# Two entries of an attention step's order exchanged: scores ahead of transposes, on one Trainium2 core

## The chip, the core and the metric

The kernel runs on one core of a Trainium2 chip. The metric is device time in microseconds of one execution, from launch to end; lower is better. Engines are named as in the profile: PE is TensorE, with PEld for its weight loads, DVE is VectorE, ACT is ScalarE, POOL is GpSimd, and SP is the engine that issues DMAs.

## What is computed

An attention with a hash mask, followed by a mixture of four two-layer networks over all rows (cut to what matters):

```python
batch, n_heads, seq, head_dim = 2, 8, 768, 64
q_bits = (q @ proj > 0); k_bits = (k @ proj > 0)          # 6 bits each
mask = q_bucket[:, :, :, None] == k_bucket[:, :, None, :]  # same 6-bit bucket
scores = where(mask, scale * q @ k.T, -1e9)
attn = exp(scores - max) / (sum + 1e-9)
x = (attn @ v), heads side by side                        # 1536 x 512
for e in range(4):
    out += p[:, e:e+1] * (relu(x @ w1[e]) @ w2[e])        # 512 -> 1024 -> 512
```

## The kernel before

**Stages.** The attention of batch 0 runs first and alone (8 heads, about the first 125 us). After it the networks run on batch 0's rows, with the attention of batch 1 spread between their matmuls, and last the networks on batch 1's rows.

**A head** has 768 rows, in 6 steps of 128 rows each. In the text, step t of head h is one of steps 0 to 5, and heads of batch 0 are 0 to 7, with head 8 the first of batch 1. One pass of the loop `for i in range(...)` in `attention()` handles step i and also late stages of earlier steps, each given by one letter of the string `ORDER`:

- **S** (`stage_s`, L447 and L449 on PE): the scores of step i, four matmuls into a double PSUM bank `sps`, of which there are two; then on DVE the row minimum and copy into the SBUF tile `p` (L454).
- **E** (`stage_e`, L470 on ACT): the exponential of step i-1, in place in `p`.
- **T** (`stage_t`, L515 on PE): the six 128x128 transposes of the tile `p` of step i-3, three into each of two PSUM banks `ptps`. ACT copies the first bank to SBUF (L521); the second is copied by DVE (L519) in steps 0, 2, 3 and 5, by ACT in steps 1 and 4. There are four single banks, shared with `pv` and `hps` below, and a bank is written again when its last reader is done. Only batch 0's heads have this stage.
- **X** and **Y**: batch 1's way to transpose, on DVE and by DMA.
- **V** (`stage_v`, L565 on PE): attention times v of the head before, one half (12 matmuls) in step 3 and one in step 5; **U** copies the result `pv` out, ACT (L592) for one half and DVE (L590) for the other, in step 2.
- **N**, **R**, **M**: the row sums' reciprocals (L481, L482 on DVE), their way through DRAM, and on POOL the scaling by them (in steps 3 and 4 of every odd head, L603 to L608).
- **P**: the preparation of the next head. Step 1: `ah` on ACT (L376) and from it three copies on POOL (L265). Step 2: `al` on DVE (L379) and from it a POOL copy `ah<-al` (L265). Step 3: hash matmuls `hps` on PE (L391), their signs on ACT (L401), then on POOL `al<-k` (L406) and `k<-al` (L265), which the first scores of the next head read.

The code is emitted in this order, and each engine executes its own instructions in the order in which they were emitted:

```python
for i in range(n + LAG_M[1] + 3):
    for op in ORDER:
        c = do(op, i)
        if c is not None:
            yield c
```

`T` and `S` each end with a `yield`. While batch 0's attention runs alone, the caller counts the yields, and on some of them puts in a piece of the split of the first weights (a DVE cast, L755, and a POOL subtraction, L745).

Of the kernel before, what the change touches and what calls it, by code (L numbers as in the profile page):

```python
# [42 lines left out]
W_SPLIT = 40  # L43
W_STEP = 6
PREP_AT = 0
ORDER = "TXSUVMEYNRP"
LIGHT_FROM = 8
DRAIN = 2000
SPLIT_FIRST = 3
# [7 lines left out]
def tile_lsh_attention__then__domain_moe(  # L57
# [570 lines left out]
    def attention():  # L628
# [76 lines left out]
# [3 lines that stand above are left out]
# [509 lines left out]
```

## Time and profile before

| | |
|---|---|
| median of 3 runs | 703.48 us (703.40 to 703.51) |
| the profiled execution | 703.57 us, of which its span is 701.9 us |
| PE busy | 695.0 us (99%) |
| DVE, ACT, POOL busy | 515.3, 330.9, 307.5 us |
| TensorE clock granted | 0.999 of full speed |

The span runs from the first to the last instruction; the rest of the time lies around it. A busy share is an average over stages. PE's ends of matmuls are modelled, so PE's waits are better read from the distance between the starts of its groups than from its busy time.

### The profile page before, as it was taken

Reading aid. Unit: us, or ns where it says so; the run is one execution under the profiler, and the core shown is the slowest. Engines: PE = TensorE matmul, PEld = TensorE weight load, DVE = VectorE, ACT = ScalarE, POOL = GpSimd, SP = SyncE. Lnnn points to the kernel's source line nnn. Section 1 sums busy time; section 2 is a strip of 40 time slices with the busy share of each in tenths; the row PEclk is TensorE's granted clock in tenths of the full one; section 3 lists DMA queues with packets and bytes.
Section 4 is the critical chain, followed back from the end, with each engine's and each line's share of the span. In section 5 each row is a group of like instructions: output and inputs, shape, how many; then the busy total and the mean of one; then the engine's idle time right before and its main releaser. Section 6 shows DMA issues by size and latency. Waiting matters only on the chain.

```text
span 701.9 us, 10122 instructions
## 1 busy us (share of the span) xinstructions
PE 695.0 (99%) x3702; PEld 589.4 (84%) x3702; DVE 515.3 (73%) x839; ACT 330.9 (47%) x646; POOL 307.5 (44%) x290
## 2 busy tenths in 40 slices
PE   8999999999999999999999999999999999999998
PEld 7766675878878878877998989899898989989896
DVE  6898898967678568785768786777767667776762
ACT  7887788544543553551424444343333424343330
POOL 6359578623443543461525555342423324232420
PEclk9999999999999999999999999999999999999999
DMA  5323444669979778684221222411123121112202
GB/s 140 67 49 75 88 105 80 233 168 295 253 224 306 219 249 296 215 289 140 60 77 52 83 70 81 149 62 62 62 87 90 50 71 61 61 60 91 81 11 90
DMA packets 83938, 87.77 MB, mean 125 GB/s; under 512 B 52400, under 2 KB 54960, under 8 KB 81840
## 3 DMA queue, kind: packets, MB, share of 16 engines
q1 hardware_dynamic: 82864, 86.79, 41.4%
q8 instruction: 29, 0.48, 0.3%
q10 hardware_dynamic: 1024, 0.33, 0.2%
q14 instruction: 21, 0.17, 0.1%
HBM read 65.04 MB, written 22.07 MB: 124 GB/s over the span
## 4 chain that ended last, share of the span: by engine, by line
PE 94%; DVE 2%; POOL 2%; issue 1%; ACT 1%; DMA 0%; POOLq 0%; DVEq 0%
PE mps L786 13%; PE mps L788 12%; PE mps L787 12%; PE mps L1070 8%; PE mps L1074 8%; PE mps L1073 8%; PE pv L565 8%; PE sps L447 4%; PE sps L449 4%; PE ptps L515 4%; PE mps L836 3%; PE mps L838 3%; PE mps L837 3%; PE hps L391 1%; DVE p L454 1%
## 5 line engine op out<-in xcount | busy, mean ns | idle before, releaser
L786 PE MATMUL mps<-w2hi,hh 128*128 128x512 f32 (+1 forms) x388 | 150.6, 388 | 0.0
L788 PE MATMUL mps<-w2hi,hl 128*128 128x512 f32 (+1 forms) x388 | 150.3, 387 | 0.0
L787 PE MATMUL mps<-w2lo,hh 128*128 128x512 f32 (+1 forms) x388 | 150.3, 387 | 0.0
L1056 POOL TENSOR_TENSOR w2lo<-ws,w2hi 128x512 fp32r<-128x512 f32 x48 | 61.2, 1298 | 148.4 <-ACT w2hi L1055 146.9
L454 DVE TENSOR_SCALAR_CACHE_REDUCE p<-sps 128x768 f32<-128x768 f32 x96 | 90.3, 941 | 27.8 <-PE sps L449 26.1
L470 ACT ACTIVATE p<-p,nb 128x768 f32<-128x768 f32 x96 | 89.5, 932 | 24.1 <-DVE p L454 23.7
L780 DVE SCALAR_TENSOR_TENSOR acc<-mps,pe,acc 128x512 f32<-128x512 f32 (+1 forms) x85 | 63.0, 741 | 45.6 <-PE mps L788 45.2
L1074 PE MATMUL mps<-xo,w1lo 128*128 128x384 f32 x272 | 91.4, 336 | 0.0
L1073 PE MATMUL mps<-xo,w1hi 128*128 128x384 f32 x272 | 91.3, 336 | 0.0
L1070 PE MATMUL mps<-xo,w1hi 128*128 128x384 f32 x272 | 91.3, 336 | 0.0
L1080 ACT ACTIVATE hh<-mps 128x384 fp32r<-128x384 f32 x96 | 47.3, 492 | 92.5 <-PE mps L1074 62.9
L788 PEld LDWEIGHTS mps<-w2hi,hl 128*128 128x128 f32 x388 | 72.9, 188 | 15.2
L786 PEld LDWEIGHTS mps<-w2hi,hh 128*128 128x128 f32 x388 | 72.9, 188 | 14.5 <-issue 0.6
L787 PEld LDWEIGHTS mps<-w2lo,hh 128*128 128x128 f32 x388 | 72.9, 188 | 14.0
L1100 DVE TENSOR_TENSOR mt<-mps,mt 128x384 f32<-128x384 f32 x72 | 40.2, 558 | 45.2 <-PE mps L1074 44.4
L1014 POOL TENSOR_TENSOR w1lo<-ws,w1hi 128x512 fp32r<-128x512 f32 x36 | 49.5, 1378 | 44.3 <-ACT w1hi L1010 17.1
L565 PE MATMUL pv<-pt,tv 128*64 128x384 f32 x288 | 67.1, 492 | 0.0
L1085 DVE SCALAR_TENSOR_TENSOR hl<-mps,hh 128x384 fp32r<-128x384 f32 x96 | 53.4, 556 | 14.7 <-ACT hh L1080 12.4
L1010 ACT ACTIVATE w1hi<-wc 128x512 fp32r<-128x512 f32 x48 | 30.0, 630 | 66.6 <-DVE wc L1019 66.6
L265 POOL TENSOR_SCALAR q<-ah 64x768 fp32r<-64x768 f32 (+1 forms) x33 | 27.1, 822 | 76.2 <-ACT ah L376 61.9
L447 PE MATMUL sps<-ah,q 128*128 128x384 f32 x192 | 54.0, 362 | 0.4 <-DVE p L454 0.4
L534 DVE STREAM_TRANSPOSE t<-p 128x768 f32<-128x768 f32 x48 | 46.2, 964 | 8.5 <-ACT p L470 8.3
(137 smaller groups left out, 1372.2 us busy)
## 6 DMA issues: line engine op xcount, KB each, us to landing
ws<-in_moe_w_dram SPq DMA_DIRECT2D x64, 512.0 KB, 3.8
scr<-t SPq DMA_DIRECT2D x16, 1152.0 KB, 8.0
pt<-scr SPq DMA_DIRECT2D x16, 1152.0 KB, 6.8
tv<-in_v_dram SPq DMA_DIRECT2D x16, 192.0 KB, 5.9
tqk<-in_q_dram SPq DMA_DIRECT2D x30, 96.0 KB, 3.6
out_dram<-acc SPq DMA_DIRECT2D x11, 256.0 KB, 2.0
tqk<-in_k_dram SPq DMA_DIRECT2D x28, 96.0 KB, 3.7
rdb<-row SPq DMA_DIRECT2D x14, 192.0 KB, 4.5
```

The lines of the kernel that those rows point to most:

```text
L447: nc.tensor.matmul(ps[:, i, :NH], q1[:, sl], k1[:, i * NH : (i + 1) * NH], start=True, stop=False)
L454: nc.vector.tensor_scalar(out=two(pt), in0=ps[:, :, :NH], scalar1=MASKED, scalar2=MASKED, op0=ALU.min, op1=ALU.min, accum_out=nb,)
L470: nc.scalar.activation(pt, pt, ACTF.Exp, bias=nb, scale=-1.0, accum_out=dens[b, h, r][:, o : o + 1])
L565: nc.tensor.matmul(dst, vvs[b, h][:, c], pts[b, h, g][c], start=c == 0, stop=c == NT - 1, tile_position=(0, g * D),)
L780: nc.vector.scalar_tensor_tensor(out=acc, in0=ps, scalar=pcol, in1=acc, op0=ALU.mult, op1=ALU.add)
L786: nc.tensor.matmul(ps, hh[:, ts], w2hi[:, f, cs], start=n == 0, stop=False)
L787: nc.tensor.matmul(ps, hh[:, ts], w2lo[:, f, cs], start=False, stop=False)
L788: nc.tensor.matmul(ps, hl[:, ts], w2hi[:, f, cs], start=False, stop=n == FC - 1)
L1056: nc.gpsimd.tensor_tensor(out=lo[:, c + o], in0=t[:, o], in1=hi[:, c + o].bitcast(F32), op=ALU.subtract)
L1070: nc.tensor.matmul(ps, whi[:, kk, fs], xh[kk], start=first and kk == 0, stop=False, skip_group_check=True)
L1073: nc.tensor.matmul(ps, whi[:, kk, fs], xl[kk], start=False, stop=False, skip_group_check=True)
L1074: nc.tensor.matmul(ps, wlo[:, kk, fs], xh[kk], start=False, stop=kk == KH - 1, skip_group_check=True)
```

## The change

The two letters T and S change places, by way of X: in each step the scores of the step now come ahead of the transposes of the tile three steps behind.

```diff
 PREP_AT = 0
-ORDER = "TXSUVMEYNRP"
+ORDER = "XSTUVMEYNRP"
 LIGHT_FROM = 8
```

Batch 1's heads have no T, and X stands ahead of S in both strings, so nothing moves there but at the border between the two batches. ACT's and POOL's instructions stand in the same order before and after, SP's too.

On PE, this is the second half of attention times v in step 5 (its last matmul), and steps 0 and 1 of the next head; before:

```order
L565 MATMUL pv<-pth,tv 64x384
L515 MATMUL ptps<-ident,p 128x128 x6
L447 MATMUL sps<-ah,q_538 128x384 x2
L449 MATMUL sps<-k_541,al 128x384 x2
L515 MATMUL ptps<-ident,p 128x128 x6
L447 MATMUL sps<-ah,q_538 128x384 x2
L449 MATMUL sps<-k_541,al 128x384 x2
```

and now:

```order
L565 MATMUL pv<-pth,tv 64x384
L447 MATMUL sps<-ah,q_538 128x384 x2
L449 MATMUL sps<-k_541,al 128x384 x2
L515 MATMUL ptps<-ident,p 128x128 x6
L447 MATMUL sps<-ah,q_538 128x384 x2
L449 MATMUL sps<-k_541,al 128x384 x2
L515 MATMUL ptps<-ident,p 128x128 x6
```

After attention times v PE had the transposes first; now it has the first scores of the new head first. The same holds behind the hash matmuls of step 3.

On DVE, this is the stretch from step 2 of a head (its minimum, L454) over the copy out of `pv` and the preparation of the next head (L590 to L379) to steps 3 and 4; before:

```order
L519 COPY pth<-ptps 128x3x128
L454 TENSOR_SCALAR p,nb<-sps 128x768
L590 COPY xr<-pv 64x384
L481 TENSOR_SCALAR den<-den 128x6
L482 RECIPROCAL rd<-den 128x6
L379 SCALAR_TENSOR_TENSOR al<-xt,qk_scale,ah 128x768
L519 COPY pt<-ptps 128x3x128
L454 TENSOR_SCALAR p,nb<-sps 128x768 x2
```

and now:

```order
L454 TENSOR_SCALAR p,nb<-sps 128x768 x2
L519 COPY pth<-ptps 128x3x128
L590 COPY xr<-pv 64x384
L481 TENSOR_SCALAR den<-den 128x6
L482 RECIPROCAL rd<-den 128x6
L379 SCALAR_TENSOR_TENSOR al<-xt,qk_scale,ah 128x768
L454 TENSOR_SCALAR p,nb<-sps 128x768
L519 COPY pt<-ptps 128x3x128
```

The copies L519 of steps 2 and 3 now stand behind the minimum L454 of their step.

## Rows read from the trace of the kernel before

**Rows 1.** Span, clock; then a window's length, busy PE, PEld, DVE, ACT, POOL, clock, DMA.

```profile
core 0: 701.9 us, clock 0.999
...
125.00:650.00 525.00, 525.00 (x2703) 460.44 (x2700) 381.90 (x589) 217.38 (x413) 213.58 (x173) 1.00 0.44 141
```

**Rows 2.** Timeline of PE in head 6: start, length, instructions merged.

```profile
86.70 0.87 PE L515 MATMUL ptps<-ident,p 128*128 128x128 f32 x6
87.33 0.59 PE L447 MATMUL sps<-ah,q 128*128 128x384 f32 x2
87.76 0.51 PE L449 MATMUL sps<-k,al 76*128 76x384 f32 x2
88.11 0.82 PE L515 MATMUL ptps<-ident,p 128*128 128x128 f32 x6
88.69 0.60 PE L447 MATMUL sps<-ah,q 128*128 128x384 f32 x2
...
91.55 0.59 PE L447 MATMUL sps<-ah,q 128*128 128x384 f32 x2
...
92.42 0.54 PE L565 MATMUL pv<-pt,tv 128*64 128x384 f32 x1
...
94.41 0.81 PE L391 MATMUL hps<-xt,pf 128*44 128x384 f32 x4
95.15 1.04 PE L515 MATMUL ptps<-ident,p 128*128 128x128 f32 x6
...
98.24 0.54 PE L565 MATMUL pv<-pt,tv 128*64 128x384 f32 x1
...
100.33 0.87 PE L515 MATMUL ptps<-ident,p 128*128 128x128 f32 x6
```

**Rows 3.** Timeline of ACT in head 6, brackets: idle time ahead.

```profile
87.28 0.49 ACT L521 ACTIVATE pth<-ptps 128x384 f32<-128x384 f32 x1 [1.19 <-PE ptps L515]
...
91.14 0.49 ACT L521 ACTIVATE pth<-ptps 128x384 f32<-128x384 f32 x1
91.52 0.48 ACT L592 ACTIVATE xr<-pv 64x384 f32<-64x384 f32 x1
```

**Rows 4.** Timeline of DVE in head 6, steps 2 and 3.

```profile
92.64 0.56 DVE L590 COPY xr<-pv 64x384 f32<-64x384 f32 x1
...
93.47 1.54 DVE L379 SCALAR_TENSOR_TENSOR al<-xt,qk_scale,ah 128x768 fp32r<-128x768 f32 x1
95.03 0.56 DVE L519 COPY pt<-ptps 128x384 f32<-128x384 f32 x1
```

**Rows 5.** Timeline of POOL: pieces of the preparation in heads 3, 5, 6, 7.

```profile
59.15 0.83 POOL L265 TENSOR_SCALAR k<-al 12x768 fp32r<-12x768 f32 x1
...
80.92 0.83 POOL L265 TENSOR_SCALAR ah<-al 64x768 fp32r<-64x768 f32 x1 [0.96 <-DVE al L379]
...
85.88 0.83 POOL L265 TENSOR_SCALAR k<-al 12x768 fp32r<-12x768 f32 x1
...
94.28 1.42 POOL L265 TENSOR_SCALAR k<-ah 64x768 fp32r<-64x768 f32 x1
...
113.47 0.83 POOL L265 TENSOR_SCALAR k<-al 12x768 fp32r<-12x768 f32 x1
```

**Rows 6.** Timeline: PE transposes at heads' starts, and ACT's copy before batch 0's last product.

```profile
17.57 0.88 PE L515 MATMUL ptps<-ident,p 128*128 128x128 f32 x6 [0.61 <-ACT p L470]
...
44.82 0.87 PE L515 MATMUL ptps<-ident,p 128*128 128x128 f32 x6
...
60.49 0.82 PE L515 MATMUL ptps<-ident,p 128*128 128x128 f32 x6
...
72.71 0.88 PE L515 MATMUL ptps<-ident,p 128*128 128x128 f32 x6
...
113.89 0.88 PE L515 MATMUL ptps<-ident,p 128*128 128x128 f32 x6
...
119.75 0.47 ACT L521 ACTIVATE pth<-ptps 128x384 f32<-128x384 f32 x1
```

## The prediction, made before the changed kernel ran

> **What bounds the kernel now.** I read the table of stages first. From 125 us to 650 us PE is busy for all of the 525 us, at a granted clock of 1.00 [rows 1], so what is gained or lost ahead of 125 us moves the end by as much. Batch 1's order does not change, so the whole question lies in the first 125 us, batch 0's attention.
>
> Next I read the timeline of PE in one head there, by the distance between starts. Write S0 and T0 for the scores and transposes of a head's step 0, and so on. A T takes 0.58 us up to the scores behind it (88.11 to 88.69), and 0.63 when it comes after attention times v (86.70 to 87.33). An S takes 0.78 up to a T (87.33 to 88.11) and 0.87 up to attention times v (91.55 to 92.42). The halves of attention times v take 1.99 (92.42 to 94.41) and 2.09 (98.24 to 100.33), the hash 0.74 [rows 2]. The head's instructions cost 4 x 0.58 + 2 x 0.63 + 4 x 0.78 + 2 x 0.87 + 4.08 + 0.74 = 13.26 us, and the head lasts 13.63 (86.70 to 100.33). So PE sets the pace with some 0.4 us of waits. One of them stands in T4, which begins at 95.15: its second bank is still being copied out by DVE until 95.59, while its first three transposes take only 0.29 us [rows 2, 4].
>
> Then I read the other engines for how near they are. ACT waits 1.19 us for T0 behind attention times v, copies at 87.28, and from there works without a break to the copy of T2, which ends at 91.63 [rows 3]. The first half of attention times v reads that copy; it starts at 92.42 [rows 2], 0.79 us later. That is all the room ACT has. DVE ends `al` at 95.01 and copies step 3's bank right behind it [rows 4]. POOL's last preparation `k<-al` ends at 59.98, 86.71 and 114.30 in heads 3, 5 and 7 [rows 5].
>
> **The change, step by step.** No instruction is added or removed; 48 groups of transposes, and their DVE copies, move behind one group of scores. What this costs in a head, from the moment at which PE leaves the head before (time 0):
>
> *PE alone.* T now goes ahead of attention times v and S behind it. I price T up to attention times v as 0.58 plus the 0.09 that S pays there, and an S behind attention times v or the hash as 0.78 plus the 0.05 that T pays there. The sum is again 13.26: the move itself is free.
>
> *ACT starts later.* S0 takes 0 to 0.83, so T0 starts at 0.83, and ACT's first copy 0.58 behind (86.70 to 87.28) at 1.41, where it was 0.58 [rows 2, 3]. ACT waited there already, so nothing absorbs this. The copy of T2 ends 4.35 later (87.28 to 91.63), at 5.76, and PE can go on about 0.06 after. PE itself arrives at 3 x (0.78 + 0.58) + 0.05 + 0.78 + 0.67 = 5.58. Attention times v begins at 5.82: a **wait of 0.24**.
>
> *DVE's copy of step 3 is later.* ACT's half of the copy of `pv` ends at 1.41 + 4.72 = 6.13 (92.00 less 87.28) and DVE's half starts after it, at 6.2 [rows 3]. `al` starts 0.83 to 1.1 after that (0.83 in the row), takes 1.54, and now a minimum of 0.88 comes between it and the copy of 0.55, which ends near 10.1 [rows 4]. PE leaves attention times v at 7.81 and the hash at 8.55, does S4 in 0.83, and needs that bank for T4's second half at 9.67. I take a **wait of 0.45**; 0 if DVE's steps keep their old times, 0.9 if a cast falls among them. The head then lasts 13.26 + 0.24 + 0.45 = **13.95**, against 13.63.
>
> *POOL's preparation is later, and is wanted sooner.* POOL's first copies need ACT's `ah`, which moves by 0.83. They then run into `al` on DVE: the copy that starts at 94.28, inside `al` (93.47 to 95.01), takes 1.42 and ends 0.69 after it, while its like takes 0.83 [rows 4, 5]. With `al` ending near 8.7, `k<-ah` ends near 9.4, and `ah<-al` starts there, not at 80.92 less 72.71, 8.21, as in head 5 [rows 5, 6]: 1.2 later. Behind it stands a fixed queue on POOL up to `k<-al`. In the odd heads it holds the scaling by the row sums too, and `k<-al` ended at 15.16, 14.00 and 13.97 (heads 3, 5, 7, from rows 5 and the starts in [rows 6]). Now it ends at 16.4, 15.2, 15.2, and the next head's S0 asks for it at 13.95 + 0.43 = 14.38 (its L449 stands 0.43 behind L447 [rows 2]), since no transposes stand ahead of it. **Waits of 2.0, 0.8 and 0.8.** Behind them T0 has still to run, where it used to fill part of the time. In even heads the queue is shorter and ends with room.
>
> The SBUF page of the Trainium skill ("SBUF — State Buffer", Who interferes with whom) gives a rule for this: DVE and GpSimd share one pair of ports as an exclusive lock, and a DVE instruction with two SBUF inputs holds it until it ends. The 1.42 agrees with it nearly; by the rule alone the blocked copy would take its full 0.83 after `al`, which makes the three waits 0.14 longer each and the sum 0.4 us larger.
>
> *Beginning and end.* In head 1 T0 waited 0.61 us for an exponential [rows 6]; S0 now goes there. I take -0.5 (0 to -0.6). At the end, batch 0's last product waits for the copy that ends at 120.22 [rows 6], at the end of an ACT queue that starts with T0 of head 8 and so moves by 0.8 again: +0.7 (0 to 0.8).
>
> **Sum.** Even heads 2, 4, 6: 3 x 0.32 = +0.96. Head 3, up to the point where S0 and T0 of head 4 are done: 13.95 + 2.0 + 1.41 less 15.67 (44.82 to 60.49) = +1.7. Head 5: 13.95 + 0.8 less 13.99 (72.71 to 86.70) = +0.8. Head 7: 13.95 + 0.8 less 13.56 (100.33 to 113.89) = +1.2 [rows 2, 6]. Beginning -0.5, end +0.7. Together **+4.8 us**. The profiled execution took 703.57, the median is 703.48, less than 0.1 apart, so I forecast 708.3.
>
> **Rivals.**
> *Faster: the waits of T go, and nothing takes their place.* A tile has one S more of time until it is transposed, which covers the waits for exponentials and copies. The same skill's page on traces ("Perfetto Trace Analysis", Optimization Strategy) tells one to find the gaps of the most contended engine and make what they wait for complete sooner, which this order does for T. With no waits, five heads fall by 0.37 each, head 5 by 0.73, head 4's start by 0.6, the beginning by 0.5: -3.7, 699.8. It comes out so if ACT ends T2's copy before PE has come to attention times v; against it, ACT has 0.79 us of room and is put back by 0.83 against PE's clock, and PE arrives earlier by 0.14. Chance 0.09.
> *No change.* New waits of about 0.4 us per head and a POOL that is not late, since in heads 6 and 7 its queue is full and not `ah` sets its times: 703.5, within 0.2% either way. For it speaks that the move itself is free; against it, head 3's `k<-al` was already late in the old order. Chance 0.13.
> *Slower by more.* DVE's casts and `al` block POOL oftener, and the delays of one head reach into the next: another 3 us or so, 711.5. Chance 0.10.
> That the change does nothing is excluded: PE's and DVE's rows are in another order.
>
> **Numbers.** The forecast's chance is 0.68. Its low end: even heads 0.1 better than before, `ah<-al` late by ACT's 0.83 alone (odd heads +1.3, +0.4, +0.8), beginning -0.6, end 0: +1.5, about 705. Its high end: 0.5 us more in each of six heads and no gain at the beginning: +8.3, 711.8. The range 704.0 to 711.3 leaves out the faster case (0.09), the part of the unchanged one below 704.0 (0.07) and an upper edge (0.04). A measurement of this kernel tells 0.2%, 1.4 us, from no change; so slower by more than that 0.78, within it 0.13, faster 0.09.
>
> **What would show it.** In the profile after, ACT's idle time for T0 behind attention times v should be near 2.0 us and not 1.19; PE should wait for ACT's copy at the first half of attention times v, for DVE's copy in T4, and for POOL's `k<-al` at S0 of heads 4, 6 and 8, by 2.0, 0.8, 0.8; heads 2, 4 and 6 should last about 13.95; and the windows behind 125 us should be the old ones, moved. I am wrong if heads last under 13.6, or if POOL is done in time: that is decided by whether POOL's first copies wait for `ah` or for POOL's own queue.

## The result and the profile after

| | before | after |
|---|---|---|
| median of 5 runs | 703.51 us (703.40 to 703.69) | 708.13 us (708.01 to 708.46) |
| span of the profiled execution | 701.9 us | 706.3 us |

The ratio is 1.0066, 95% interval 1.0051 to 1.0081: the change makes the kernel 4.6 us slower.

The window behind 125 us in the kernel after comes first, as in [rows 1]: its length, then busy time and count of PE, PEld, DVE, ACT and POOL, the granted clock, DMA share and rate. Below it stands the first matmul of the networks, after and then before.

```profile
125.00:650.00 525.00, 525.00 (x2700) 458.02 (x2697) 382.51 (x592) 217.91 (x415) 215.61 (x175) 1.00 0.44 140
...
129.83 0.44 PE L836 MATMUL mps<-xs,w1hi 128*128 128x384 f32 x1
...
125.44 0.44 PE L836 MATMUL mps<-xs,w1hi 128*128 128x384 f32 x1
```

The window reads as it did: PE full, clock 1.00. The first matmul of the networks begins at 129.83 us where it began at 125.44. These 4.4 us are the whole growth of the span, so all of the loss is in batch 0's attention.

Next is PE's timeline in head 6 of the kernel after, which answers to [rows 2] (start, length, instructions merged, and in brackets idle time and its releaser).

```profile
89.06 0.62 PE L447 MATMUL sps<-ah,q 128*128 128x384 f32 x2
...
90.07 0.82 PE L515 MATMUL ptps<-ident,p 128*128 128x128 f32 x6
...
94.14 0.49 PE L515 MATMUL ptps<-ident,p 128*128 128x128 f32 x3
94.99 0.55 PE L515 MATMUL ptps<-ident,p 128*128 128x128 f32 x3 [0.36 <-ACT pth L521]
...
99.01 0.83 PE L515 MATMUL ptps<-ident,p 128*128 128x128 f32 x6
99.59 0.60 PE L447 MATMUL sps<-ah,q 128*128 128x384 f32 x2
...
103.22 0.61 PE L447 MATMUL sps<-ah,q 128*128 128x384 f32 x2
```

The head lasts 14.16 us (89.06 to 103.22) against 13.63 before. T0 begins 1.01 us behind the head's start, 0.20 of it a wait of S0 for POOL (shown below for head 4). T3 now breaks in two: its second half has to wait until ACT has copied the bank that it goes to. T4 runs through here; in most of the heads it waits.

The same head on ACT and then on DVE, which answers to [rows 3, 4].

```profile
90.60 0.49 ACT L521 ACTIVATE pth<-ptps 128x384 f32<-128x384 f32 x1 [2.03 <-PE ptps L515]
...
94.45 0.49 ACT L521 ACTIVATE pth<-ptps 128x384 f32<-128x384 f32 x1
94.83 0.48 ACT L592 ACTIVATE xr<-pv 64x384 f32<-64x384 f32 x1
```

```profile
95.40 0.56 DVE L590 COPY xr<-pv 64x384 f32<-64x384 f32 x1
...
96.23 1.54 DVE L379 SCALAR_TENSOR_TENSOR al<-xt,qk_scale,ah 128x768 fp32r<-128x768 f32 x1
97.80 0.96 DVE L454 TENSOR_SCALAR_CACHE_REDUCE p<-sps 128x768 f32<-128x768 f32 x1
...
98.68 0.55 DVE L519 COPY pt<-ptps 128x384 f32<-128x384 f32 x1
```

ACT waits 2.03 us for T0 where it waited 1.19. Its copy out of `pv` ends at 95.31, and DVE's copy out of `pv` starts right behind it, 6.34 us into the head (5.94 before). So `al` starts 7.17 us into the head, where it was 6.77. After `al` the minimum comes first and step 3's copy second.

Last, the first scores of head 4, on PE and on POOL.

```profile
59.80 0.62 PE L447 MATMUL sps<-ah,q 128*128 128x384 f32 x2
61.44 0.62 PE L449 MATMUL sps<-k,al 76*128 76x384 f32 x2 [1.02 <-POOL k L265]
```

```profile
60.55 0.83 POOL L265 TENSOR_SCALAR k<-al 12x768 fp32r<-12x768 f32 x1
```

`k<-al` ends at 61.38, 15.90 us into head 3 (45.48 to 59.80). Its half of the scores stands 1.64 behind L447 and not 0.45: a wait of some 1.2 to 1.3 us. At heads 6 and 8 the same wait is 0.20 and 0.14.

Counted from the end of one head's attention times v to the next, the lengths of heads 2 to 7 went from 13.63, 13.64, 14.25, 13.99, 13.63 and 13.56 to 14.83, 14.32, 15.02, 14.24, 14.16 and 14.27.

### The profile page after: what moved, and what is told of

It reads as the page before. It is cut to its first block, busy times and chain, and to the rows that moved or that the text cites. A ratio compares the mean times of both kernels' runs of the same rounds, so it can differ in the third digit from the quotient of the medians.

```text
span 706.3 us, 10131 instructions
## 1 busy us (share of the span) xinstructions
PE 696.1 (99%) x3702; PEld 591.5 (84%) x3702; DVE 512.9 (73%) x839; ACT 331.4 (47%) x646; POOL 309.0 (44%) x290
## 4 chain that ended last, share of the span: by engine, by line
PE 90%; ACT 4%; DVE 3%; issue 1%; POOL 1%; DMA 0%; POOLq 0%; ACTq 0%
PE mps L786 12%; PE mps L788 12%; PE mps L787 12%; PE mps L1070 8%; PE mps L1074 8%; PE mps L1073 8%; PE pv L565 8%; PE sps L447 4%; PE sps L449 4%; PE mps L836 3%; PE mps L838 3%; PE mps L837 3%; PE ptps L515 2%; ACT p L470 2%; DVE p L454 1%
## 5 line engine op out<-in xcount | busy, mean ns | idle before, releaser
L454 DVE TENSOR_SCALAR_CACHE_REDUCE p<-sps 128x768 f32<-128x768 f32 x96 | 90.2, 942 | 31.6 <-PE sps L449 30.4
L788 PEld LDWEIGHTS mps<-w2hi,hl 128*128 128x128 f32 x388 | 72.9, 188 | 15.2
L447 PE MATMUL sps<-ah,q 128*128 128x384 f32 x192 | 54.6, 364 | 0.4 <-DVE p L454 0.4
```

Of the source, the lines that this page charges most:

```text
L447: nc.tensor.matmul(ps[:, i, :NH], q1[:, sl], k1[:, i * NH : (i + 1) * NH], start=True, stop=False)
L454: nc.vector.tensor_scalar(out=two(pt), in0=ps[:, :, :NH], scalar1=MASKED, scalar2=MASKED, op0=ALU.min, op1=ALU.min, accum_out=nb,)
L788: nc.tensor.matmul(ps, hl[:, ts], w2hi[:, f, cs], start=False, stop=n == FC - 1)
```

## The experiments

All were timed in 5 rounds against the kernel before, whose medians beside them were 703.63 to 703.85. Six of them are the kernel before with the new order in some steps of each head only:

```diff
+S_FIRST = (1, 2, 3, 4, 5)
+ORDER_S = "XSTUVMEYNRP"
...
-            for op in ORDER:
+            for op in ORDER_S if i % NT in S_FIRST else ORDER:
```

| steps in the new order | us | ratio, 95% interval |
|---|---|---|
| 0 | 709.49 | 1.0082 (1.0068 to 1.0096) |
| 1, 2 | 708.15 | 1.0065 (1.0051 to 1.0078) |
| 3 | 707.70 | 1.0061 (1.0049 to 1.0074) |
| 4, 5 | 703.43 | 0.9996 (0.9987 to 1.0004) |
| 3, 4, 5 | 703.52 | 1.0000 (0.9992 to 1.0009) |
| 1 to 5 | 707.54 | 1.0053 (1.0041 to 1.0066) |
| all | 708.13 | 1.0066 (1.0051 to 1.0081) |

The parts don't add: step 3 alone costs 4 us, and together with 4 and 5 it costs nothing.

**Steps 1 to 5.** My first theory was that ACT's start behind S0 makes the loss.

> Scores first in steps 1 to 5 of a head, transposes first in step 0, right behind attention times v. My theory (the cost starts with ACT, which gets its first copy of a head one S later): ACT's idle time ahead of that copy goes back from 2.03 to about 1.2 us, the wait in T3 (0.57 us in four heads) and most of that in T4 go, POOL's k<-al is ready when it is wanted except in head 4: 701 to 704 us. Rival (the cost is DVE's copies standing behind the minima of steps 2, 3 and 5, whatever step 0 does): the waits in T3 and T4 stay, 706 to 708 us.

It came out at 707.54, in the rival's range, and the theory fell. The rival's reason doesn't hold either: steps 3 to 5, further down, have the minima first and cost nothing. ACT's timeline in head 5 of this kernel shows why the loss stays.

```profile
75.36 0.49 ACT L523 ACTIVATE pth<-ptps 128x384 f32<-128x384 f32 x1 [1.09 <-PE ptps L517]
...
77.43 0.87 ACT L523 ACTIVATE pth<-ptps 128x384 f32<-128x384 f32 x2 [0.66 <-PE ptps L517]
```

T0 is early again, but S0 and S1 then stand together, T1 comes an S later, and ACT waits for that instead. From there it is as late as in the kernel after: `al` starts 7.22 us into this head (7.26 after, 6.64 before).

**Step 0 alone**, `S_FIRST = (0,)`.

> Scores first in step 0 alone, transposes first in steps 1 to 5. My theory: most of the loss is here by itself, since ACT's copies, ah, DVE's al and POOL's k<-al of every head come 0.8 us later: 706 to 708.5 us. Rival (DVE's order in steps 2, 3 and 5): about the time before, 703 to 704.5 us.

It gave 709.49, a microsecond above the range: slower than all steps together. T0 and T1 now follow one another, which takes 0.22 us more per head, and `al` starts 7.21 us into head 5; which of its waits makes it slower than all steps together is not shown.

**Steps 1 and 2**, `S_FIRST = (1, 2)`.

> Scores first in steps 1 and 2 alone, so that T3 follows T2 with no scores between. My theory: ACT's copies are as late as in the changed kernel while T3 comes an S sooner, so that T3 waits about 1.2 us in each head: 708 to 712 us, worse than the changed kernel. Rival (steps 1 and 2 have no part in the loss): 703 to 705 us.

708.15, as the theory had it. T2 and T3 stand together, with 0.84 to 0.93 us of waits in five heads and 1.36 in head 6, where 1.2 was forecast. But what the trace names ahead of T3 in most heads is an exponential on ACT and a copy on DVE, not ACT's copy.

**Steps 4 and 5**, `S_FIRST = (4, 5)`, and **steps 3 to 5**, `S_FIRST = (3, 4, 5)`.

> Scores first in steps 4 and 5 alone. My theory: ACT, `al` and the copy of step 3 keep their old times, T4 comes an S later and its waits (0.17 to 0.23 us in each head before) go: 701.5 to 703 us, at or under the kernel before. Rival (each S ahead of a T costs, wherever it stands): 704.5 us or more.

> Scores first in steps 3, 4 and 5, transposes first in 0, 1 and 2, so that PE goes from T2 through S2 and S3 to T3. Since the run with step 0 alone put back was the changed kernel again from T1 on, my theory is now that the loss starts where ACT's copies of T1 and T2 come an S later, in whichever step the S is put ahead, with T3's second bank and `al` waiting behind them. Then here T3's wait (0.57) is gone, `al` is at its old time, and only the minimum ahead of the copy of step 3 is left, about 0.2 us in T4: 702 to 704 us. Rival (the minima ahead of the copies on DVE cost by themselves): T4 waits 0.4 us or more, 705 to 707 us.

703.43 and 703.52: neither differs from no change. The waits of the old order in T4 or T5 (0.17 to 0.23 us per head) go in the first, but 0.71 us come in head 2, where S5 waits for a minimum that stands on DVE behind the sums for the networks' weights, and S0's wait for POOL at head 4 is 0.79 and not 0.62. So the copy of step 3 behind the minimum costs nothing, if what comes ahead of it is on time.

**Step 3 alone**, `S_FIRST = (3,)`.

> Scores first in step 3 alone. My theory: the copy of step 3 stands behind the minimum on DVE and T4 comes first after the hash, so that T4's second bank waits about 1.0 us in each head, 0.8 more than before: 707 to 710 us. Rival (the minimum ahead of the copy is harmless, as DVE has idle time): 703 to 705 us.

707.70. Head 5 of that kernel on PE and on DVE:

```profile
74.47 0.77 PE L517 MATMUL ptps<-ident,p 128*128 128x128 f32 x5
...
82.84 0.55 PE L517 MATMUL ptps<-ident,p 128*128 128x128 f32 x3
84.06 0.55 PE L517 MATMUL ptps<-ident,p 128*128 128x128 f32 x3 [0.67 <-DVE pt L521]
...
88.69 0.77 PE L517 MATMUL ptps<-ident,p 128*128 128x128 f32 x5
```

```profile
81.10 1.43 DVE L381 SCALAR_TENSOR_TENSOR al<-xt,qk_scale,ah 128x768 fp32r<-128x768 f32 x1
...
83.45 0.55 DVE L521 COPY pt<-ptps 128x384 f32<-128x384 f32 x1
```

And head 5 of the kernel with steps 3 to 5, in the same way:

```profile
72.25 0.87 PE L517 MATMUL ptps<-ident,p 128*128 128x128 f32 x6
...
81.43 0.95 PE L517 MATMUL ptps<-ident,p 128*128 128x128 f32 x6
82.13 0.59 PE L449 MATMUL sps<-ah,q 128*128 128x384 f32 x2
...
85.75 0.87 PE L517 MATMUL ptps<-ident,p 128*128 128x128 f32 x6
```

```profile
78.88 1.43 DVE L381 SCALAR_TENSOR_TENSOR al<-xt,qk_scale,ah 128x768 fp32r<-128x768 f32 x1
...
81.22 0.55 DVE L521 COPY pt<-ptps 128x384 f32<-128x384 f32 x1
```

`al` starts at 6.63 us in both heads. The copy starts 2.35 and 2.34 behind it, and T4's second half 2.96 behind `al` (84.06) and about the same in the second kernel (82.13 less the 0.3 that three transposes take: 2.95). What differs is what is left: 4.63 us with S4, S5, T5 and the second half of attention times v (84.06 to 88.69), 3.92 where S4 has already run (81.83 to 85.75). So a head of the new order lasts, by this chain, **the start of `al` + 2.95 + 3.92**: 13.50 here, which is what the head lasts (72.25 to 85.75). In the kernel after `al` starts 7.26 us into head 5 and 7.17 into head 6, which gives 14.13 and 14.04, and 0.11 more since `al` takes 1.54 there and not 1.43: 14.24 and 14.15. They last 14.24 and 14.16. With the start and the length of each head's own `al`, the same sum comes within 0.02 us of the length of every head from 3 to 7 (in head 2 other work on DVE comes in between) in five kernels that have steps 3 to 5 in the new order: steps 3 to 5, steps 1 to 5, the kernel after, and the two below that leave out the scaling or give T3 another bank.

**POOL.** Whether POOL's queue makes the loss: the multiplication by the row sums' reciprocals (L603) is left out for batch 0, whose outputs are therefore not normalised, in both orders.

```diff
-        nc.gpsimd.tensor_tensor(out=x3, in0=x3, in1=rdb, op=ALU.mult)
+        if b:
+            nc.gpsimd.tensor_tensor(out=x3, in0=x3, in1=rdb, op=ALU.mult)
```

In the new order:

> The changed order, with batch 0's scaling by the row sums on POOL left out (16 POOL instructions of 1.2 us; the rows stay unnormalised). My theory: the waits of PE for POOL's k<-al at S0 of heads 4, 6 and 8 (1.3, 0.2, 0.14 us in the trace after) go and nothing takes their place: 1.2 to 1.7 us less than the changed kernel, 706.4 to 707.0 us. Rival (PE would wait for ACT or DVE at the same place anyway): no more than 0.5 us less.

In the old one:

> The order of before, with the same scaling left out. My theory: the one wait for POOL in the old order (0.62 us at S0 of head 4) goes: 702.8 to 703.1 us, so that POOL's part of the whole loss is the difference of the two, 0.6 to 1.1 us of 4.6. Rival (POOL bears most of the loss): the two orders come within 2 us of each other without it.

They gave 707.59 and 703.13 (ratios 1.0056, 1.0043 to 1.0068, and 0.9995, 0.9986 to 1.0003). The new order gains 0.54, the old one about as much. Neither is clear of the spread of the times, but by the traces heads 2 to 7 together are 0.53 and 0.54 us shorter. So the 1.2 to 1.7 us of the theory did not come, though in the new order all three waits at S0 go, 1.6 us. PE's rows in head 4 of the first kernel show where it went.

```profile
60.13 0.63 PE L447 MATMUL sps<-ah,q 128*128 128x384 f32 x2
60.60 0.52 PE L449 MATMUL sps<-k,al 76*128 76x384 f32 x2
60.96 0.82 PE L515 MATMUL ptps<-ident,p 128*128 128x128 f32 x6
...
69.47 0.49 PE L515 MATMUL ptps<-ident,p 128*128 128x128 f32 x3
70.50 0.55 PE L515 MATMUL ptps<-ident,p 128*128 128x128 f32 x3 [0.54 <-DVE pt L519]
```

S0 runs through, and T4 waits 0.75 us for DVE where it waited 0.20 (in the same place T4 takes 1.33 instead of 0.77). POOL's waits were real, but most of them stood in for a wait that comes later in the head. The chain says the same: `al` starts 7.30 us into this head where it started 8.16, and takes 1.55 instead of 1.41, which makes it 0.72 shorter; it lasts 14.29 and not 15.02.

**T3's bank.** That is a claim about any wait ahead of T4, so I tested it with one that has nothing to do with POOL. In heads 2, 3, 5 and 6 of the kernel after, T3's second half goes into the bank that ACT copies last; in heads 4 and 7, as in heads 2 to 7 before, into one that DVE has copied. The kernel below leaves the order of every instruction as it is and only names the four single banks by a list, with two of them exchanged there.

```diff
-    ps1 = ctx.enter_context(tc.tile_pool(name="ps1", bufs=4, space=PSUM))
+    ps1 = ctx.enter_context(tc.tile_pool(name="ps1", bufs=1, space=PSUM))
+    next_bank = iter(BANKS)
...
-        return ps1.tile([P, 512], F32, tag="one", name=name)
+        return ps1.tile([P, 512], F32, tag="one" + next(next_bank), name=name)
```

> New order, the same instructions in the same order on every engine; only the four single PSUM banks are named by a list, taken from the changed kernel, in which two banks exchange their places at T3 of heads 2, 3, 5 and 6, so that T3's second half goes into the bank that DVE has copied out and not into the one that ACT copies last. Both theories: the pitch of T3 in these heads falls from 1.33 us to 0.85 to 0.90, as in head 4. Theory 1 (the wait in T3 is a loss of its own): 4 x 0.43 less, 706.2 to 706.6. Theory 2 (DVE's copy of step 3, which follows from ACT's start and not from PE, sets when T4 can go on, and T4 waits for longer by what T3 waits for less): at least half comes back, 707.3 to 708.2, and the pitch of T4 in heads 3, 5 and 6 rises by 0.3 to 0.4.

It took 708.33 us (ratio 1.0061, 1.0048 to 1.0075). PE's rows of T3 and T4 in head 2, in the kernel after and then in this one:

```profile
35.53 0.49 PE L515 MATMUL ptps<-ident,p 128*128 128x128 f32 x3
36.38 0.55 PE L515 MATMUL ptps<-ident,p 128*128 128x128 f32 x3 [0.36 <-ACT pth L521]
...
40.40 0.49 PE L515 MATMUL ptps<-ident,p 128*128 128x128 f32 x3
41.55 0.55 PE L515 MATMUL ptps<-ident,p 128*128 128x128 f32 x3 [0.67 <-DVE pt L519]
```

```profile
35.71 0.96 PE L522 MATMUL ptps<-ident,p 128*128 128x128 f32 x6
36.60 0.54 PE L572 MATMUL pv<-pt,tv 128*64 128x384 f32 x1
...
40.14 0.49 PE L522 MATMUL ptps<-ident,p 128*128 128x128 f32 x3
41.74 0.55 PE L522 MATMUL ptps<-ident,p 128*128 128x128 f32 x3 [1.11 <-DVE pt L526]
```

Up to the start of attention times v T3 takes 0.89 us (35.71 to 36.60) and not 1.32 (35.53 to 36.85), where it would be 0.75 with no wait, as for T5 in head 6 of the kernel after (100.38 to 101.13). T4's halves stand 1.60 apart and not 1.15. What T3 gave, 0.43, T4 took, 0.45. It is so in heads 3 (0.43 and 0.44) and 5 (0.44 and 0.45) as well, and head 6 lasts 14.16 in both kernels. All of it comes back, and the time lies 0.1 us above the second theory's range, which had asked for half at least. So the second theory holds: T3's wait costs nothing of its own.

**Both banks of T2 copied by DVE**, in the new order, to take the late copy off ACT.

```diff
-            if i and o % 2 == 0:
+            if i and o % 2 == 0 or t == NT - 1:
```

> New order throughout, but DVE and not ACT copies the first bank of T2 out (7 copies of 0.49 us leave ACT, 7 of 0.55 go to DVE). Theory (ACT's copy of T2, late by one S, holds a bank that T3 needs in four heads): the wait of 0.58 us in T3 of heads 2, 3, 5 and 6 goes, ACT's copy out of pv starts 0.5 earlier, and the time comes 2 to 4 us below 708.13, at 704 to 706. Rival (the time at which DVE reaches al decides): DVE has 0.55 more ahead of al, al comes no sooner, T4's wait grows to about 1 us per head, and the time is 707.5 or more.

It took 710.79 (1.0102, 1.0088 to 1.0116), which the rival's range holds. T3's wait fell as expected, and heads 3, 4 and 7 last as long as in the kernel after all the same (14.34, 15.01 and 14.26). The time rose by things neither side had named. PE in head 6 and at the end of batch 0, then ACT in head 6:

```profile
94.05 0.96 PE L515 MATMUL ptps<-ident,p 128*128 128x128 f32 x6
96.18 0.54 PE L565 MATMUL pv<-pt,tv 128*64 128x384 f32 x1 [1.17 <-ACT pt L521]
...
127.42 0.54 PE L565 MATMUL pv<-pth,tv 128*64 128x384 f32 x1 [1.73 <-DVE pth L519]
```

```profile
95.65 0.47 ACT L521 ACTIVATE pt<-ptps 128x384 f32<-128x384 f32 x1
```

The result of attention times v got the bank of T3's own first half, in heads 5 and 6, and waits for ACT's copy of that. Each of the two waits for 1.2 us or more there, and lasts 0.80 and 0.59 us longer than in the kernel after. The larger part stands at the end of the batch: there the copy that DVE took over comes behind a transpose and a minimum of batch 1, and attention times v waits 1.73 us for it, so that head 8's start and the networks are 14.31 us apart and not 12.34. Head 2 alone is shorter, by 0.78. So this run doesn't say whether relief for ACT alone would help.

**A version to beat both.** Steps 4 and 5, and the first nine passes, in the new order; and the same with the split of the first weights begun five passes later.

```diff
+            for op in ORDER_S if i < 9 or i % NT in S_FIRST else ORDER:
...
-W_SPLIT = 40
+W_SPLIT = 45
```

> Scores first in steps 4 and 5 of every head and in the first nine passes (head 0 and half of head 1), transposes first elsewhere. If the gain at the beginning (0.5 us, where T0 of head 1 waits for an exponential) adds to the -0.1 of steps 4 and 5: 702.8 to 703.2. Rival (what is gained early is lost at the next wait in head 2, where a minimum on DVE stands behind the work on the weights' split): 703.4 to 703.7.

> As the one before, and the batch's first split of weights starts at pass 45 of the count and not 40, so that the casts on DVE fall behind other steps. If the wait of 0.7 us in head 2 comes from them: 702.0 to 702.8. Rival (the casts block other steps as much): 703 or more.

703.75 and 703.49, beside 703.85 of the kernel before (ratios 1.0000 and 0.9998, 0.9989 to 1.0007 for the second). The second does lose the 0.71 us in head 2, but T3 of head 4 then waits as long for DVE (0.72), and the networks begin at 125.02 instead of 125.44 without the span being shorter by more than 0.1. I found nothing better than the order before.

## Why the prediction came out

The sum, +4.8, was near the +4.6 measured (4.4 in the profiled execution), and the mechanism is the one it rests on: S0 ahead of T0 makes ACT, then DVE, then T4 late. That it came so near is in part luck, since two errors in its terms cancel. They came out like this, by the traces:

| term | predicted | measured |
|---|---|---|
| beginning | -0.5 | -0.54 |
| head 2 | +0.32 | +1.20 |
| head 3 to T0 of head 4 | +1.7 | +1.33 |
| rest of head 4 | +0.32 | +0.1 |
| head 5, with S0 of head 6 | +0.8 | +0.45 |
| rest of head 6 | +0.32 | +0.33 |
| head 7, with S0 of head 8 | +1.2 | +0.85 |
| end | +0.7 | +0.65 |

*PE alone.* Right in the main: steps 4 and 5, or 3 to 5, in the new order change nothing, so the exchange itself is free there. But T ahead of attention times v was priced too low: it takes 0.75 us (100.38 to 101.13) and not 0.67, so that PE's own sum for a head is near 13.4 and not 13.26. The 13.63 of the old order has room for that.

*ACT starts later.* Right: T0 comes an S0 later and nothing absorbs it. The 2.03 us of idle time where 2.0 was forecast holds S0's wait of 0.20 for POOL; in the heads without such a wait it is 1.76 to 1.84. The wait that follows was to be 0.24, at attention times v. In heads 4 and 7 it is there, with 0.15 and 0.10; in heads 2, 3, 5 and 6 it stands in T3 instead, with 0.58, by the bank that T3 gets. I had not looked at which bank the new order hands out.

*DVE's copy of step 3.* Right in its times: DVE's half of the copy out of `pv` at 6.34 (6.2), `al` 0.83 behind, the copy of 0.55 that begins at 9.62 and was to end near 10.1. T4's waits are 0.88, 0.38, 0.20, 0.30, 0.01 and 0.81 in heads 2 to 7, 0.43 on average, against 0.45, but no head lies near that average save head 3. Head 2's is larger because three small operations for the networks' weights stand on DVE between the minimum and the copy, which I had not priced.

*POOL.* This is the term that was mis-sized: 2.0, 0.8 and 0.8 became 1.29, 0.20 and 0.14. `k<-al` ended at 15.90, 14.74 and 14.71 us into heads 3, 5 and 7 (forecast 16.4, 15.2, 15.2), and the heads lasted 14.2 to 14.3, so that it was also asked for later than at 13.95. The step that fails is that `al` holds up `k<-ah`: in heads 3, 5 and 7 `k<-ah` began 0.07 to 0.09 us ahead of `al` and took its 0.83, and `k<-al` came 0.74 later than before and not 1.2. The smaller POOL terms and the larger head 2 cancel in the sum.

*What the sum itself got wrong* is that waits were added. The experiments on POOL and on T3's bank took away 1.6 and 1.6 us of waits, and the time fell by 0.5 and by nothing: a head's length follows from when `al` ends, and the waits ahead of T4 share out the same room. Within a head the forecast had this right, since it took T4's 0.45 from the end of DVE's copy and with the 0.24 already in it; what it added on top in full is POOL's waits. The forecast's low end also adds up to +1.6 and not +1.5, which moves nothing.

Of the rivals, "faster" failed where it was said to: ACT is not done before PE comes. "No change" had POOL's queue in time, which it nearly was, at heads 6 and 8; it failed on DVE's chain. "Slower by more" had `al` block POOL oftener: `k<-ah` was held up in heads 4 and 6 only, where no S0 came to wait for it. What stays open is why the parts of the change taken alone cost almost as much as all of it: for step 3 the chain shows it, but steps 0, or 1 and 2, make new neighbours of their own (T0 beside T1, T2 beside T3), and I did not separate these from the late `al`. That this lateness makes the loss wherever steps 3 to 5 have the new order is shown by the sum that fits five such kernels.

## What to carry to other kernels

When engines with fixed queues hand work around a loop, an exchange on the busiest engine is judged by the start of what the next engine waits for, followed once round, here T0, ACT's copies and `ah`, `al`, step 3's copy and T4, and not by the waits that it removes. Waits that lie ahead of the point where such a chain comes back are not to be added up: taking one away here filled another, in part or in full. And if a pool hands out buffers by their order of use, a change of order also changes who must be done with them; look that up for every head, not for one.

## What the runs showed that I had not expected

DVE's `al` and POOL's copies of `ah` hold each other up, and which of them waits depends here on which began first. First POOL's and DVE's rows in head 4 of the kernel after, then ACT's, POOL's and DVE's in head 5, and at the end head 5 of the kernel before:

```profile
66.83 1.73 POOL L265 TENSOR_SCALAR q<-ah 64x768 fp32r<-64x768 f32 x2
68.64 1.42 POOL L265 TENSOR_SCALAR k<-ah 64x768 fp32r<-64x768 f32 x1
...
67.96 1.41 DVE L379 SCALAR_TENSOR_TENSOR al<-xt,qk_scale,ah 128x768 fp32r<-128x768 f32 x1
```

```profile
79.18 0.93 ACT L376 ACTIVATE ah<-xt,qk_scale 128x768 fp32r<-128x768 f32 x1
...
81.99 0.83 POOL L265 TENSOR_SCALAR k<-ah 64x768 fp32r<-64x768 f32 x1
...
82.08 1.54 DVE L379 SCALAR_TENSOR_TENSOR al<-xt,qk_scale,ah 128x768 fp32r<-128x768 f32 x1
```

```profile
76.33 0.93 ACT L376 ACTIVATE ah<-xt,qk_scale 128x768 fp32r<-128x768 f32 x1
...
79.13 0.83 POOL L265 TENSOR_SCALAR k<-ah 64x768 fp32r<-64x768 f32 x1
...
79.35 1.42 DVE L379 SCALAR_TENSOR_TENSOR al<-xt,qk_scale,ah 128x768 fp32r<-128x768 f32 x1
```

In head 4 `al` begins in the second of the two copies `q<-ah`. They end at 68.56, and `al` ends 0.81 us after that, at 69.37. The copy `k<-ah` that begins inside `al` ends 0.69 after it (70.06). In head 5 `k<-ah` begins 0.09 ahead of `al` and keeps its 0.83, and `al` ends 0.80 after it (82.82 and 83.62). The same 0.80 or 0.81 stands between the end of the copy that runs when `al` begins and the end of `al` in all of heads 2 to 7 of the kernel after. So the time of `al` alone can be put at 0.8 us, an estimate from these rows, and what its row shows beyond that, 0.6 and 0.74 us here, is a wait for POOL. The Trainium skill's page "SBUF — State Buffer" (Who interferes with whom) says that whichever of the two engines issues first gets the shared ports for its whole instruction and the other is blocked. The rows agree both ways, but that the copy behind `al` comes 0.14 us sooner than its full 0.83.

This says how ACT's late start reaches `al` in head 5. The copies on POOL need ACT's `ah`, which ends 5.29 us into the head and not 4.55, so that `k<-ah` ends 0.75 later (8.00 and 7.25), and `al` 0.74 later (8.80 and 8.06). It is so in heads 2, 3 and 7 as well. DVE's copy out of `pv` and what follows it set when `al` begins, but in these heads not when it ends. That is also what shortened head 2 in the kernel with both banks of T2 copied by DVE: `al` began while a copy `q<-ah` ran, ahead of `k<-ah`, and ended 7.89 us into the head and not 8.81.
